# Edge copies of three batches on ScalarE, a new order of emission, and six fewer filler matmuls

## The chip, the core and the metric

The kernel runs on one core of a Trainium2 chip. The time is the device time of one launch in microseconds: the median of 3 runs. The engines of the core are TensorE (PE in the rows, with its weight loads as PEld), VectorE (DVE), ScalarE (ACT), GpSimd (POOL) and SyncE (SP), which issues most of the DMA transfers. Each engine works off its own list of instructions in order; between engines they wait for one another by semaphores.

## What is computed

Eight batches of eight heads, 512 tokens, 32 states and 64 columns to a head. Tokens attend to states and states to tokens; both results go through a feed-forward layer whose hidden values are gated by a convolution of width 3 along the tokens.

```python
scores = scale * np.matmul(x, state.transpose(0, 1, 3, 2))
a = softmax(scores)
xread = np.matmul(a, state)
scores2 = scale * np.matmul(state, x.transpose(0, 1, 3, 2))
a2 = softmax(scores2)
sread = np.matmul(a2, x)
x = np.concatenate([xread, sread], axis=2)      # 576 rows to a batch, 512 columns
...
h = np.maximum(x @ w_in, 0.0)                   # 576 x 1024
hp = h with one row of zeros on either side
for k in range(3):
    conv_out += conv_w[k][None, None, :] * hp[:, k:k + S, :]
gate = 1.0 / (1.0 + np.exp(-conv_out))
return h * gate @ w_out
```

## The kernel before

Hidden values are held with the 1024 columns on partitions, as eight blocks `f` of 128 for each batch `b`; a step `i` is one pair (`b`, `f`) of 512 tokens. For a step TensorE makes `ps_h` (`first_hidden` for batch 0, `hidden` for the others), `relu` copies it into the tile `h`, `middle` multiplies by the convolution's middle tap into `t`, two instructions of VectorE add the outer taps (`before`, `behind`), ScalarE takes tanh (`sigmoid`), VectorE gates (`gate`), `gate_high` and `gate_low` split the result into two parts for TensorE, and `project` adds them into `acc` with three matmuls to a 128-token chunk. `end` scales an `acc` into `o`, and `store` sends it off. All stores go on SP's queue but one, `LAST`, which goes on ScalarE's.

The 32 state rows of a batch stand behind its 512 tokens. They are computed for four batches at once: `state_tokens` fills `hs`, which holds them for each block with a column of space on either side. Two copies join the two parts: `join` copies the first state column behind the tokens of `h` (column 512), and `edge` copies the last token column in front of the states in `hs`. Both are 128x1 copies on GpSimd. Batch 0 comes before its states are there, so its very last token column is finished later: `edge` also keeps the last two columns of each block in `corner`, and `corner_taps`, `corner_sum` and what follows make the missing column, which is then in `last`. A buffer of `h` is free for a later step when `join`, `edge`, the taps and the gate of its step are through; there are five of them, and eight PSUM banks in all.

Batch 0 is also started in a shorter way: `first_scores` multiplies the states `st` (loaded by `state_load`, the first part on ScalarE's DMA queue) with the first half of the tokens `xt`, and then the second half; `keep_scores` keeps them, `first_flip` transposes them, `first_top` takes the maximum, and so on to `first_div`, before `first_hidden` can begin. Weights are rounded on ScalarE and VectorE as they come (`w_abs` to `w_sign`), the convolution's weights `conv_w` (the DMA of `w_load` on ScalarE's queue, then `raw` and `hc`) among the first.

`fill` is a matmul of zeros that nobody reads. What stands in which order is not computed in the kernel: every operation is added to a plan with what it reads and writes, and the table `ORDER` lists their numbers in the order in which they are emitted. A number -n stands for n calls of `fill`, and a number with a v for an operation that VectorE takes in place of ScalarE. Tile numbers in the lists below (`h_1098`) count the tiles as they are made.

Of the kernel before, what the change touches and what calls it, by code (L numbers as in the profile page):

```python
# [12 lines left out]
AF = mybir.ActivationFunctionType  # L13
# [3 lines left out]
B, H, S, NS, D = 8, 8, 512, 32, 64  # L17
# [28 lines left out]
LAST = (B - 1, 1, 1)  # L46
# [37 lines left out]
876 863 396 890 943v 864 738 891 973 877 1521 324 946 309 957 843 879 858 892 392 958 894 311 932 840 325 865 441 855  # L84
# [3 lines left out]
1044 1526 448 952 481 482 966 1527 479 475 1029v 937 480 477 1528 999 478 1030 941 940 923 1010 955 938 956 924 1529  # L88
# [6 lines left out]
1123 1138 1066 408 1094 1139v 1142 1140 1155 414 409 1067 1079 1168 1069 1068 1080 1537 1095 1082 1083 1158 1143 1107  # L95
1124 1539 1127v 1108 1144 1540 1169 1145 1146 1172 1159 1109 1170 1084 1097 1099 1098 1081 1110 1541 1251 374 1156 377
1173 1171 1141 1174 1125 1252 1126 1112 1114 1117v 378 375 1118 1147 1148 376 1542 1530 1128 1538 1266 1096 1113 1129
1160 1121 1130 1543 1161 1131 1175 1162 1111 1176 1183 1544 1132 1177 1267 1115v 1184 1198 1178 1187v 1199 1254 1202v
1201 1122 1203 1545 1133 1547 1213 1228 1546 1136 1200 1204 1255 1256 1548 1163 1205 1270 1137 1134 1149 1135 1253
1185 1188 1189 1206 1257 1549 1150 1152 1550 1258 1551 1190 1116 1119 1120 1191 1214v 1167 1192 1552 1182 1164 1151  # L100
1179 1166 1553 1181 1207 1217v 1216 1186 1193 1555 1215 1268 1229 1196 1165 1194 1296 415 1556 1259 1218 1232v 1271
1219 1208 1211 1272 1220 1297 1180 1209 1230 1233 1557 1558 1559 1560 1234 1554 1195 1221 416 418 1222 1273 1223 1561
1235 1281 1197 1210 1236 1300 1237 1282v 1231 1284 417 419 1274 1298 1238 1285 1212 1226 1224 1227 1225 1269 1240 1311
1241 1563 1275 449 1301 1302 1312 1299 1286 1283 1326 1242 1247 1287 1288 1248 1289 1356 1290 1303 1239 1315v 1276
1327v 1304 1260 1243 1341 1261 1342 1343 1357v 1313 1344 1314 1329 1358 1249v 1316 1244 456 1317 1564 1250 451 1359
1305 452 454 457 1565 1291 1263 1278 1264 1562 1279 1294 1566 455 1567 453 1568 1569 1330v 1345 1570 1346 450 459 1571
1572 1573 1360 1262 1318 1319 1277 1293 1292 1379 460 1361 1306 1574 1362 1575 1309 1265 1347 1280 1308 1576 1577 1380
1363 1381 458 1331 1364 1578 1584 1382 1328 1383 1320 1579 1332 1585 1384 1348 1333 1586 1321 1580 1582 1245v 1334
1587 1335 1588 1246 1581 1385 1424 1394 1295 1589 1386 1425 1336 1590 1387 1409 1349 1428 1307 1324 1429 1323 1310
1350 1410 1365 1351 1338 1325 1427 1411 1395v 1396 1340 1412 1397 1339 1366 1583 1322 1592 1593 1398 1413v 1399 1414  # L110
1594 1415 1416 1439 1595 1596 1597 1400 1426 1430 1598 1401 1440 1600 1441 1402 1601 1469 1337 1602 1603 1431 1388
1604 1591 1605 1432 1606 1389 1353 1454 1455 1484 1458v 1403 1417 1456 1485v 1459 1352 1354 1355 1393 1608 1609 1610
1404 1470v 1472 1599 1368 1370 1611 1607 1418 1392 1419 1460 1443 1612 1457 1444 1442 1613 1471 1473v 1373 1488 1369
# [46 lines left out]
def fused_kernel(ctx: ExitStack, tc: tile.TileContext, xT, xn, stT, w_in, conv_w, w_out, out):  # L160
# [478 lines left out]
    def relu(i, on=A):  # L639
        hd[i] = buf([P, S + 1], F32, "h", f"h_{i}")  # L640
        rectified(hd[i][:, :S], ps_h.pop(i), on)

    def join(i):
        b, f = at_step(i)
        m, j = PLACE[b]
        G.tensor_copy(hd[i][:, S:], hs[m, f][:, j, 1:2])  # L646
# [293 lines left out]
```

## Time and profile before

| | |
|---|---|
| median of 3 runs | 360.16 us (359.75 to 360.31) |
| the profiled execution | 359.77 us |
| its span in the trace | 358.0 us |
| outside the span | 1.77 us |
| instructions | 6754 |

The times compare whole launches; the rows of the profile stand within the span of the one profiled execution. The profile lists for each engine how long its instructions ran, in which stretch, and, in brackets, how long the engine had been idle before an instruction and which other instruction let it go on. Matmuls overlap with one another, so the time of a group of them is best read from its start to the start of the next group.

### The profile page before, as it was taken

To read this page: it belongs to the slowest core of one execution; us is meant where nothing else is said; L and a number is where in the kernel's file an instruction comes from. 1 tells how busy PE (TensorE), PEld (TensorE's weight loads), DVE (VectorE), ACT (ScalarE), POOL (GpSimd) and SP (SyncE) were. 2 spreads that over 40 slices of the span, in tenths; PEclk is the share of its full clock that TensorE was granted. 3 is DMA by queue.
4 is the path that set the end of the run, shared out by engine and by line. 5 is a ranking of instruction groups with operands and counts; after the bars stand their busy time and mean duration, and the time that the engine had idled before them with its cause. 6 is when DMAs were issued, how large, how long until landed. Compare 5 with 4: busy or idle time off the path is not lost.

```text
span 358.0 us, 6754 instructions
## 1 busy us (share of the span) xinstructions
PE 351.5 (98%) x2556; PEld 274.9 (77%) x2556; DVE 319.0 (89%) x566; ACT 251.0 (70%) x517; POOL 45.3 (13%) x144
## 2 busy tenths in 40 slices
PE   8999999999999999999999999999999999999995
PEld 6867667857778787878789886887887868888884
DVE  1999999989999999999999999998888699989850
ACT  3999999879768789668867469455746575755532
POOL 1012020152010102000101003030110210204000
PEclk9999999999999999999999999999999999999999
DMA  7999999500200014031600011001000020200114
GB/s 233 384 351 335 369 356 305 205 0 32 89 2 0 3 59 146 2 117 39 231 0 2 0 44 75 0 2 57 34 29 0 13 77 0 61 0 0 60 60 147
DMA packets 13584, 35.06 MB, mean 98 GB/s; under 512 B 1520, under 2 KB 4720, under 8 KB 12528
## 3 DMA queue, kind: packets, MB, share of 16 engines
q1 hardware_dynamic: 13120, 34.41, 26.9%
q8 instruction: 20, 0.33, 0.4%
q10 hardware_dynamic: 432, 0.22, 0.2%
q14 instruction: 12, 0.10, 0.1%
HBM read 25.71 MB, written 8.91 MB: 97 GB/s over the span
## 4 chain that ended last, share of the span: by engine, by line
PE 90%; ACT 5%; DMA 2%; POOL 1%; issue 0%; SPq 0%
PE acc L694 47%; PE ps_h L629 20%; PE ps_hs L614 4%; PE ps_u L547 4%; PE acc_t L694 3%; PE ps_r L367 2%; DMA xt<-xT 2%; PE ps_t L354 2%; PE acc_c L694 2%; PE acc L702 1%; POOL hs L651 1%; PE idle L214 1%; ACT h L199 1%; PE ps_s L309 1%; PE ps_h L636 1%; ACT t L193 1%
## 5 line engine op out<-in xcount | busy, mean ns | idle before, releaser
L694 PE MATMUL acc<-wo,g 128*128 128x512 f32 x726 | 178.1, 394 | 0.0
L694 PEld LDWEIGHTS acc<-wo,g 128*128 128x128 f32 x726 | 134.4, 188 | 33.4 <-issue 4.2
L629 PE MATMUL ps_h<-a,u 128*128 128x512 f32 x336 | 82.9, 391 | 0.0
L629 PEld LDWEIGHTS ps_h<-a,u 128*128 128x128 f32 x336 | 62.8, 188 | 13.9 <-ACT g L204 0.8
L651 POOL COPY hs<-h 128x1 f32<-128x1 f32 x64 | 26.2, 423 | 224.4 <-ACT h L199 183.4
L671 ACT ACTIVATE t<-t 128x512 f32<-128x512 f32 x64 | 39.5, 633 | 20.9 <-DVE t L667 20.7
L667 DVE SCALAR_TENSOR_TENSOR t<-h,cw,t 128x512 f32<-128x512 f32 (+1 forms) x64 | 47.3, 745 | 1.3
L662 DVE SCALAR_TENSOR_TENSOR t<-h,cw,t 128x511 f32<-128x511 f32 x64 | 47.0, 743 | 0.5 <-ACT t L193 0.5
L676 DVE SCALAR_TENSOR_TENSOR t<-t,h 128x512 f32<-128x512 f32 (+1 forms) x64 | 41.9, 668 | 5.4 <-ACT t L671 5.3
L199 ACT ACTIVATE h<-ps_h 128x512 f32<-128x512 f32 x55 | 32.4, 594 | 18.7 <-PE ps_h L629 16.5
L204 ACT ACTIVATE g<-t 128x512 fp32r<-128x512 f32 (+1 forms) x62 | 38.0, 618 | 10.1 <-DVE t L676 8.5
L207 DVE TENSOR_TENSOR g<-t,g 128x512 fp32r<-128x512 f32 (+1 forms) x62 | 41.4, 672 | 2.3 <-ACT g L204 2.1
L193 ACT ACTIVATE t<-h,cw 128x512 f32<-128x512 f32 x53 | 37.8, 723 | 2.4 <-DVE g L207 1.3
L646 POOL COPY h<-hs 128x1 f32<-128x1 f32 x56 | 17.3, 330 | 61.4 <-DVE t L676 31.2
L204 ACT ACTIVATE u<-ps_u 128x512 fp32r<-128x512 f32 x28 | 16.4, 602 | 4.9 <-PE ps_u L547 4.9
L708 ACT ACTIVATE o<-acc 128x512 f32<-128x512 f32 (+1 forms) x27 | 14.6, 548 | 7.3 <-PE acc L694 5.9
L207 DVE TENSOR_TENSOR u<-ps_u,u 128x512 fp32r<-128x512 f32 x28 | 19.0, 683 | 0.5 <-ACT u L204 0.5
L547 PE MATMUL ps_u<-wi,st 64*32 64x512 f32 x224 | 16.0, 598 | 0.3 <-ACT h L199 0.3
L614 PEld LDWEIGHTS ps_hs<-sr,wi 128*128 128x128 f32 x128 | 14.8, 192 | 1.1 <-ACT o L708 0.8
L636 PE MATMUL ps_h<-p,u 128*128 128x256 f32 x64 | 15.4, 386 | 0.0
L614 PE MATMUL ps_hs<-sr,wi 128*128 128x128 f32 x128 | 15.0, 276 | 0.0
L636 PEld LDWEIGHTS ps_h<-p,u 128*128 128x128 f32 x64 | 11.7, 190 | 3.7 <-issue 1.3
(96 smaller groups left out, 401.0 us busy)
## 6 DMA issues: line engine op xcount, KB each, us to landing
xt<-xT SPq DMA_DIRECT2D x16, 512.0 KB, 7.6
xx<-xn SPq DMA_DIRECT2D x8, 1024.0 KB, 6.5
out<-o SPq DMA_DIRECT2D x27, 256.0 KB, 2.0
raw<-w_in SPq DMA_DIRECT2D x8, 512.0 KB, 7.7
raw<-w_out SPq DMA_DIRECT2D x8, 512.0 KB, 7.4
out<-o SPq DMA_DIRECT2D x7, 128.0 KB, 1.8
out<-o_t SPq DMA_DIRECT2D x8, 64.0 KB, 1.7
st<-stT SPq DMA_DIRECT2D x1, 448.0 KB, 10.7
```

What stands on the lines that cost most here:

```text
L193: A.activation(dst, src, AF.Copy, scale=scale)
L199: A.activation(dst, src, AF.Relu, scale=0.5)
L204: A.activation(hi, src, AF.Copy)
L207: engine.tensor_tensor(lo, src, hi.bitcast(F32), op=ALU.subtract)
L614: PE.matmul(ps_hs[m, f][:, :NT], wi[:, k, f * P:(f + 1) * P], sr[m][:, k, :], start=(k == 0), stop=(k == NK - 1))
L629: PE.matmul(ps_h[i], u[j][:, g, fs], a[k][:, g, :], start=(n == 0), stop=(n == 3 * NG - 1))
L636: PE.matmul(ps_h[f][:, q * HS:(q + 1) * HS], us[0, f // 4][0][:, g, f % 4 * P:(f % 4 + 1) * P], half_of(pa[0], q)[:, g, :], start=(g == 0) ...
L662: V.scalar_tensor_tensor(t[:, 1:], h[:, :S - 1], cw[:, f, 0:1], t[:, 1:], op0=ALU.mult, op1=ALU.add)
L667: V.scalar_tensor_tensor(t[:, :n], h[:, 1:n + 1], cw[:, f, 2:3], t[:, :n], op0=ALU.mult, op1=ALU.add)
L671: A.activation(tt[i], tt[i], AF.Tanh, scale=0.25)
L676: V.scalar_tensor_tensor(tt[i][:, :n], tt[i][:, :n], 1.0, hd[i][:, :n], op0=ALU.add, op1=ALU.mult)
L694: PE.matmul(acc, g[j][:, cs], wo[:, k, f, :], start=(f == 0 and n == 0), stop=(f == NF - 1 and n == 2))
```

## The change

`join` and `edge` of the batches 0 to 2 (`EARLY`) run on ScalarE as activations with the function Copy. For batch 0 `edge` keeps only the two `corner` columns; the copies into `hs` that it made before are made for all eight blocks at once by `first_edges` on GpSimd, as one 128x8 copy, and `corner_taps` is one such copy too. `LAST` names another store. The table `ORDER` is replaced throughout; its numbers behind step 7 are larger by one, for the new operation. The sum of its negative numbers goes from 25 to 19. Counted over the whole program, some work changes engine between ScalarE and VectorE by the table's v and by the order: VectorE has 2 in place of 0 of the four first `keep_scores` (128x256), 12 in place of 9 `relu`, 15 in place of 11 `middle`, and 4 in place of 6 whole evacuations `o`; ScalarE has the complement of each.

```diff
-LAST = (B - 1, 1, 1)
+LAST = (B - 1, 0, 0)
+
+EARLY = 3
...
 ORDER = """
-0 98 99 101 100 102 120 -9 123 121 -3 124 125 103 142 2 143 126 -2 150 127 4 3 151 5 132 20 21 23 144 152 8 22 6 24
...
+98 100 99 101 0 102 120 -9 123 121 103 -3 124 125v 126 -1 142 143 127 2 -1 150 3 151 5 132 4 144 6 152 20 128 130 21
...
+    def moved(dst, src, b):
+        if b < EARLY:
+            A.activation(dst, src, AF.Copy)
+        else:
+            G.tensor_copy(dst, src)
+
     def join(i):
         b, f = at_step(i)
         m, j = PLACE[b]
-        G.tensor_copy(hd[i][:, S:], hs[m, f][:, j, 1:2])
+        moved(hd[i][:, S:], hs[m, f][:, j, 1:2], b)
 
     def edge(i):
         b, f = at_step(i)
         m, j = PLACE[b]
-        G.tensor_copy(hs[m, f][:, j, :1], hd[i][:, S - 1:S])
         if b == 0:
-            G.tensor_copy(corner[:, f, :2], hd[i][:, S - 2:S])
+            moved(corner[:, f, :2], hd[i][:, S - 2:S], b)
+        else:
+            moved(hs[m, f][:, j, :1], hd[i][:, S - 1:S], b)
+
+    def first_edges():
+        G.tensor_copy(every[:, :NF, 0, 0], corner[:, :, 1])
...
     def corner_taps():
-        for f in range(NF):
-            G.tensor_copy(corner[:, f, 2:], hs[0, f][:, 0, 1:2])
+        G.tensor_copy(corner[:, :, 2], every[:, :NF, 0, 1])
...
+        copies = ("ACT", "small") if b < EARLY else ("POOL", "pool")
         if b:
-            add("POOL", "pool", partial(join, i), r=[("hs", m, f), h], w=[("h2", i)])
-        add("POOL", "pool", partial(edge, i), r=[h], w=[("edge", i)] + ([("corner", f)] if b == 0 else []))
+            add(*copies, partial(join, i), r=[("hs", m, f), h], w=[("h2", i)])
+        add(*copies, partial(edge, i), r=[h], w=[("edge", i)] if b else [("corner", f)])
+        if i == NF - 1:
+            add("POOL", "pool", first_edges, r=[("corner", f) for f in range(NF)] + [("hs", 0, f) for f in range(NF)],
+                w=[("edge", f) for f in range(NF)])
```

ScalarE's list at its start, before (`st` are the states, `raw` and `hc` the convolution's weights, `at` the first scores):

```order
L880 DMA st<-stT 128x128
L238 DMA raw_92<-conv_w 128x48
L242 ACT_TABLE_LOAD
L242 ACTIVATE hc_94<-raw_92 128x24
L245 ACTIVATE raw_92<-raw_92 128x24
L193 ACTIVATE at_111<-ps_s_0_0_112 128x256
L193 ACTIVATE at_111<-ps_s_0_1_113 128x256
L193 ACTIVATE at_111<-ps_s_1_0_127 128x256
```

and the same list in the changed kernel:

```order
L240 DMA raw_91<-conv_w 128x48
L247 ACT_TABLE_LOAD
L247 ACTIVATE raw_91<-raw_91 128x24
L244 ACTIVATE hc_94<-raw_91 128x24
L895 DMA st<-stT 128x128
L195 ACTIVATE at_111<-ps_s_1_0_128 128x256
L195 ACTIVATE at_111<-ps_s_1_1_129 128x256
```

The load of `st` has moved from the first place behind the two activations that read `conv_w`, and the first two copies of scores have left for VectorE.

GpSimd's list where the copies of batch 0 end and those of batch 1 begin, before (`h_1067` is the first step of batch 1 in this list, `h_696`, `h_698` and `h_667` are of batch 0):

```order
L651 COPY hs<-h_698 128x1
L653 COPY corner<-h_698 128x2
L651 COPY hs<-h_1067 128x1
L651 COPY hs<-h_696 128x1
L653 COPY corner<-h_696 128x2
L769 COPY corner<-hs 128x1 x8
L651 COPY hs<-h_667 128x1
L653 COPY corner<-h_667 128x2
```

and GpSimd's list of the changed kernel from the last instruction of its start on:

```order
L182 TENSOR_SCALAR eight<-ident 128x128
L665 COPY hs<-corner 128x8
L780 COPY corner<-hs 128x8
L649 COPY hs<-h_1876 128x1
L649 COPY h_1876<-hs 128x1
```

Before the first copies of batch 3 (`h_1876`) GpSimd has only the two 128x8 copies left.

ScalarE's list at the same place, before (each `h` takes its buffer from an earlier step):

```order
L204 ACTIVATE g_5_1080<-t_960 128x384
L199 ACTIVATE h_1086<-ps_h_1073 128x512
L204 ACTIVATE wo<-whole_1054 128x512
L199 ACTIVATE h_1098<-ps_h_1088 128x512
L671 ACTIVATE t_1012<-t_1012 128x512
L204 ACTIVATE wo<-whole_648 128x512
```

and in the changed kernel, at the last of the eight copies of batch 0:

```order
L201 ACTIVATE h_1073<-ps_h_1018 128x512
L620 ACTIVATE hs<-ps_hs_6_966 128x4x32
L647 ACTIVATE corner<-h_663 128x2
L244 ACTIVATE hc_1108<-raw_1096 128x512
L206 ACTIVATE wo<-whole_714 128x512
L206 ACTIVATE wo<-whole_1069 128x512
```

The copy of the edge now stands in ScalarE's own list, where before the next `relu` of that list stood behind a copy on GpSimd.

## Rows read from the trace of the kernel before

**Rows 1.** The page's first part: busy time, share of the span and instructions of each engine.

```profile
PE 351.5 (98%) x2556; PEld 274.9 (77%) x2556; DVE 319.0 (89%) x566; ACT 251.0 (70%) x517; POOL 45.3 (13%) x144
```

**Rows 2.** Busy time by stretch: the stretch and its length, then for each engine its busy us and instructions, the granted TensorE clock, the share of the DMA engines' time and GB/s.

```profile
20.60:70.00 49.40, 48.81 (x567) 36.23 (x560) 47.05 (x94) 47.27 (x107) 5.75 (x12) 1.00 0.92 331
70.00:78.00 8.00, 7.71 (x54) 4.30 (x53) 6.65 (x14) 5.86 (x12) 6.12 (x14) 1.00 0.00 0
78.00:130.00 52.00, 52.00 (x337) 39.68 (x336) 51.53 (x83) 42.42 (x82) 4.79 (x22) 1.00 0.07 27
130.00:340.00 210.00, 210.00 (x1248) 167.92 (x1247) 195.39 (x335) 136.20 (x275) 27.30 (x88) 1.00 0.12 43
```

**Rows 3.** The timeline from 70 to 78 us: start, us, engine, line, operation, tiles, shape, count, and in brackets the idle time before it and what ended that.

```profile
70.49 4.70 POOL L651 COPY hs<-h 128x1 f32<-128x1 f32 x2 [19.01 <-ACT h L199]
...
74.46 0.68 DVE L207 TENSOR_TENSOR wo<-whole,wo 128x512 fp32r<-128x512 f32 x1
...
74.68 1.02 PE L547 MATMUL ps_u<-wi,st 64*32 64x512 f32 x2
...
75.12 0.19 POOL L653 COPY corner<-h 128x2 f32<-128x2 f32 x1
...
75.34 0.60 ACT L199 ACTIVATE h<-ps_h 128x512 f32<-128x512 f32 x1 [1.80 <-POOL corner L653]
...
75.99 1.09 PE L547 MATMUL ps_u<-wi,st 64*32 64x512 f32 x14 [0.29 <-ACT h L199]
...
76.49 0.56 DVE L676 SCALAR_TENSOR_TENSOR t<-t,h 128x384 f32<-128x384 f32 x1 [1.35 <-ACT t L671]
...
77.01 1.20 PE L694 MATMUL acc<-wo,g 128*128 128x512 f32 x4
```

**Rows 4.** The timeline from 121 to 123 us, TensorE: the same 16 state products later, and the group behind them.

```profile
121.11 1.09 PE L547 MATMUL ps_u<-wi,st 64*32 64x512 f32 x16
...
122.13 1.20 PE L629 MATMUL ps_h<-a,u 128*128 128x512 f32 x4
```

**Rows 5.** Statistics of GpSimd's copies over the run: shortest, median and longest in ns, first and last start. The second row is that of the eight copies of `corner_taps`.

```profile
L651 POOL COPY hs<-h x64: 178/185/4002, 23.6 to 329.5; 128x1 f32<-128x1 f32 x64
...
L769 POOL COPY corner<-hs x8: 177/178/178, 75.2 to 76.1; 128x1 f32<-128x1 f32 x8
```

**Rows 6.** The timeline of the first 9 us.

```profile
0.72 0.38 ACTq L880 DMA_DIRECT2D st<-stT  x1
...
1.03 4.21 PE L214 MATMUL idle<-zeros 128*128 128x128 f32 x18 [1.03 <-DVE zeros L176]
1.14 0.45 ACTq L238 DMA_DIRECT2D raw<-conv_w  x1
...
4.90 0.22 ACT L242 ACTIVATE hc<-raw 128x24 f32<-128x24 f32 x1 [2.00 <-DMA raw<-conv_w]
5.03 0.21 ACT L245 ACTIVATE raw<-raw 128x24 uint32<-128x24 uint32 x1
...
5.41 0.67 PE L319 MATMUL ps_s<-xt,st 64*32 64x256 f32 x16 [0.16 <-DMA xt<-xT]
...
6.00 0.94 PE L214 MATMUL idle<-zeros 128*128 128x128 f32 x6
...
7.35 0.67 PE L319 MATMUL ps_s<-xt,st 64*32 64x256 f32 x16 [0.41 <-DMA xt<-xT]
...
8.64 0.69 DVE L491 TENSOR_REDUCE m<-ps_x 128x16 f32<-128x512 f32 x1 [2.58 <-PE ps_x L487]
```

**Rows 7.** DMA issues on ScalarE's queue: count, KB each, us from issue to landing.

```profile
st<-stT ACTq DMA_DIRECT2D x1, 64.0 KB, 3.0
raw<-conv_w ACTq DMA_DIRECT2D x1, 24.0 KB, 3.7
```

**Rows 8.** The timeline from 11.5 to 21 us: VectorE's wait behind the sums of the first exponentials, and TensorE's first hidden product.

```profile
14.92 0.17 DVE L515 TENSOR_SCALAR s<-ps_x 128x16 f32<-128x16 f32 x1 [0.35 <-PE ps_x L511]
...
20.59 0.70 PE L636 MATMUL ps_h<-p,u 128*128 128x256 f32 x2
```

**Rows 9.** The timeline from 36 to 41 us.

```profile
37.76 0.73 PEld L636 LDWEIGHTS ps_h<-p,u 128*128 128x128 f32 x4 [0.84 <-ACT raw L245]
...
39.47 1.10 PE L367 MATMUL ps_r<-xx,e2t 128*32 128x64 f32 x64 [0.59 <-ACT at L193]
```

**Rows 10.** Groups of instructions by line and shape: busy us, mean ns of one, and the idle time before them with what ended it.

```profile
L193 ACT ACTIVATE t<-h,cw 128x512 f32<-128x512 f32 x53 | 37.8, 723 | 2.4 <-DVE g L207 1.3 <-DVE h L201 0.9
L199 ACT ACTIVATE h<-ps_h 128x512 f32<-128x512 f32 x55 | 32.4, 594 | 18.7 <-PE ps_h L629 16.5 <-POOL corner L653 1.8 <-PE ps_h L636 0.4
...
L201 DVE TENSOR_SCALAR h<-ps_h 128x512 f32<-128x512 f32 x9 | 6.2, 686 | 0.9 <-PE ps_h L629 0.9
...
L195 DVE TENSOR_SCALAR t<-h,cw 128x512 f32<-128x512 f32 x11 | 5.3, 483 | 0.6 <-ACT h L199 0.6
...
L193 ACT ACTIVATE at<-ps_s 128x256 f32<-128x256 f32 x4 | 1.3, 380 | 2.2 <-PE ps_s L319 2.2
...
L710 DVE TENSOR_SCALAR o<-acc 128x256 f32<-128x256 f32 x2 | 0.8, 420 | 4.7 <-PE acc L694 4.7
```

**Rows 11.** The timeline of the last 4 us, ScalarE's evacuations and its store.

```profile
354.08 0.66 ACT L708 ACTIVATE o<-acc 128x256 f32<-128x256 f32 x2 [1.20 <-PE acc L694]
...
354.77 0.36 ACTq L729 DMA_DIRECT2D out<-o  x1
```

More of the change, by code (lines that the diff above doesn't have):

```diff
@@ L56 @@
 ORDER = """
[27 rows of a table removed]
-876 863 396 890 943v 864 738 891 973 877 1521 324 946 309 957 843 879 858 892 392 958 894 311 932 840 325 865 441 855
[3 rows of a table removed]
-1044 1526 448 952 481 482 966 1527 479 475 1029v 937 480 477 1528 999 478 1030 941 940 923 1010 955 938 956 924 1529
[6 rows of a table removed]
-1123 1138 1066 408 1094 1139v 1142 1140 1155 414 409 1067 1079 1168 1069 1068 1080 1537 1095 1082 1083 1158 1143 1107
-1124 1539 1127v 1108 1144 1540 1169 1145 1146 1172 1159 1109 1170 1084 1097 1099 1098 1081 1110 1541 1251 374 1156 377
-1173 1171 1141 1174 1125 1252 1126 1112 1114 1117v 378 375 1118 1147 1148 376 1542 1530 1128 1538 1266 1096 1113 1129
@@ L98 @@
[L98 to L112, printed above, removed]
@@ L113 @@
-1404 1470v 1472 1599 1368 1370 1611 1607 1418 1392 1419 1460 1443 1612 1457 1444 1442 1613 1471 1473v 1373 1488 1369
-1408 1391 1487 1486 1445 1446 1407 1489 1614 1461 1624 1423 1390 1405 1422 1420 1367 1447 1490 1625 1615 1626 1627
-1628 1629 1433 1630 1462 1616 1617 1434 1438 1618 1406 1619 1377v 1620 1621 1491 1378 1374 1474 1475 1622 1435 1421
-1437 1448 1463 1623 1449 1464 1450 1631 1492 1632 1476 1477 1633 1478 1634 1375 1635 1436 1636 1465 1453 1468 1637
-1452 1638 1376 1639 1467 1493 1640 1641 1494 1479 1642 1371v 1643 1644 1483 1645 1372 1646 1498 1511 1482 1647 1497
@@ L118 @@
-1451 1480 1509 1648 1512 1510 1650 1651 1649 1495 1499v 1513 1507v 1501 1514 1508 1502 1652 1500 1466 1481 1496 1503
-1504 1505 1506
+98 100 99 101 0 102 120 -9 123 121 103 -3 124 125v 126 -1 142 143 127 2 -1 150 3 151 5 132 4 144 6 152 20 128 130 21
[3 rows of a table added]
+137 536 537 504 158 138 159 470 161 494 472 207 519v 471 538 162 520 213 208 590 545 62 63 163 212 495 521 546 575 591
[22 rows of a table added]
+931 860 921 395 959 960 310 392 903 933 891 922 892 881 311 900 880 306 944 312 930 904 962v 973 934 861 863 326 441
[9 rows of a table added]
+1051 1105v 1055 1124 1052 1091 1077 414 1063 1540 1541 1064 1092 1542 1125 1078 1065 1139 1140 1066 1079 1142 1141
@@ new lines @@
+1093 1039 1154 1054 1106 1080 1081 412 1094 1107 1095 1155 1053 1070 1169 1068 1170v 1158v 1096 1157 1126 1127 1108
+1128v 1543 408 1171 1104 374 1129 1069 1083 1067 1173 1159 1156 375 377 1174 378 1175 1109 1130 1110 1131 1098 1084
+1544 1111 1082 409 1132 376 1545 1546 1097 1085 1099 1100 1143 1114 1144 1115 1112 1145 1116v 991 1117 1146 1548 1549
+1184 1550 1133 1176 1551 1552 1160 1185 1134 1229 1161 1199 1214 1122 449 1200v 1177 1203v 1147 1113 1148 1123 1215
+1553 1162 1216 1149 1118v 1554 1163 1252 1188 1230v 1164 1556 1178 1187 1202 1179 1297 1136 1135 415 1151 1172 1201
@@ new lines @@
+1186 1298v 1218v 1219 1220 1204 1150 1165 418 1547 1557 1189 1555 1558 416 1221 1120 1121 1190 1233v 1119 1217 1191
+1559 1137 1152 1167 1166 417 1222 1253v 1205 419 1256 1299 1254 1560 1234 1561 1206 1231 1267 1138 1153 1192 1257 1562
+1207 1235 1168 1181 1182 1183 1268 1193 1180 1258 1236 1282 1194 1283 1270 1232 1312 1208 1271v 1237 1209 1300 1286v
+1313v 1314 1238 1255 1285 1284 1223 1239 1224 1272 1269 1197 1273 1287 1288 1274 1564 1275 1198 1565 1566 1196 1327
+1213 1195 1567 1259 1289 1210 1212 1225 1276 1240 1316 1317 1228 1243 1342 1211 1568 1260 1226 1227 1357 1563 1261
@@ new lines @@
+1244 450 1343v 1262 1290 1328 1331 1277 1245 1263 1250 1569 1358 1251 1361v 1362 1291 1570 1301 1302 1303 1292 451
+1329 1330 1344 1572 1315 1345 1359 456 1242 454 452 455 1248 1573 453 1574 1332 1363 1241 457 459 1571 1575 1265 1278
+1304 1346v 1576 1246 1305 1306 1577 1280 1264 1293 1395 1347 1307 1295 1380 1578 460 1318 1381v 1585 1319 1320 1382
+1383 1586 1384 1385 1425 1266 1310 1247 1587 1348 1333 1386 1281 458 1364 1321 1334 1335 1349 1588 1589 1322 1350
+1426v 1279 1351 1294 1296 1579 1308 1410 1311 1309 1326 1411v 1590 1396v 1427 1429 1365 1591 1336 1580 1366 1583 1412
@@ new lines @@
+1398 1323 1592 1593 1387 1352 1430 1337 1428 1399v 1388 1594 1431 1414 1415 1595 1596 1581 1325 1324 1340 1339 1455
+1397 1360 1354 1355 1597 1338 1367 1598 1416 1389 1353 1249 1413 1599 1440 1601 1417 1390 1602 1368 1370 1400 1603
+1604 1441 1442 1401 1418 1605 1369 1606 1456 1459 1432 1444v 1607 1376v 1377 1582 1445 1458 1609 1402 1470 1471 1610
+1472 1473 1443 1611 1392 1433 1341 1600 1608 1393 1612 1446 1356 1447 1374 1613 1460 1614 1448 1485 1457 1419 1371
+1403 1615 1616 1391 1625 1461 1626 1404 1627 1394 1628 1629 1462 1405 1630 1407 1408 1406 1631 1617 1420 1618 1619
@@ new lines @@
+1375 1486v 1488 1422 1409 1424 1620 1434 1463 1435 1474v 1378 1621 1439 1423 1437 1464 1449 1622 1465 1623 1624 1633
+1438 1450 1452 1634 1635 1475 1421 1632 1436 1379 1487 1636 1637 1638 1639 1489 1451 1640 1453 1490 1641 1454 1584
+1491 1469 1642 1476 1492 1643 1493 1477 1644 1478 1645 1646 1647 1479 1494 1648 1372v 1649 1652 1650 1467 1468 1495
+1480 1373 1653 1466 1483 1482 1497 1651 1504 1498 1484 1506 1510v 1505 1511 1499 1508 1514v 1512 1507 1515 1513 1481
+1496 1509 1502 1500 1503 1501
```

69 rows, old and new, of the table ORDER are left out of this document.

## The prediction

> **What bounds the kernel now.** The engine totals come first [rows 1]: TensorE is busy in 98% of the span and VectorE in 89%, so a change of this kind can win only where TensorE stands, or where a run of its matmuls takes longer than its size asks for. The table by stage [rows 2] shows how little visible standing there is: after the first hidden product, which starts at 20.59 us [rows 8], TensorE is busy 48.81 of 49.40 us, then 7.71 of 8.00, then without a gap to 340. VectorE is just as full up to 130 us (51.53 of 52.00) and has 210.00 - 195.39 = 14.6 us free between 130 and 340. So TensorE sets the end, and VectorE, which prepares its operands, sets how early TensorE can go on in the first third. GpSimd, ScalarE after 70 us and the DMA queues after 70 us have room.
>
> A "busy" TensorE can hide a wait, so the next view is the timeline of the one stage where TensorE, VectorE and ScalarE all have gaps, 70 to 78 us [rows 3]. Two one-element-wide copies on GpSimd start at 70.49 and last until 75.19. The columns of such a copy are tiny, and the statistics of that line say what is normal: 185 ns in the median, 4002 ns at the longest [rows 5]. The next GpSimd copy, at 75.12, is what ScalarE's `relu` at 75.34 waited for (1.80 us idle). That `relu` gives a PSUM bank back: TensorE's group of 16 state products begins at 74.68 with 2 matmuls and goes on with the other 14 only at 75.99; the next group starts at 77.01, 2.33 us after the first matmul. The same group elsewhere needs 122.13 - 121.11 = 1.02 us [rows 4]. So TensorE lost 2.33 - 1.02 = 1.31 us there, though the waits show only 0.29. VectorE idles at the same place: its last instruction ended at 74.46 + 0.68 = 75.14 and the next, at 76.49, waited 1.35 us for ScalarE's tanh, which stands behind that `relu`. TensorE, VectorE and ScalarE all lose some 1.3 us to one late GpSimd copy.
>
> **What the rows say about the slow copy, and a rule.** It ran while VectorE worked without a gap, and it ended when VectorE stopped at 75.14 [rows 3]; the eight copies right after it, with VectorE idle, took 178 ns each [rows 5]. I take it that VectorE's back-to-back work holds GpSimd off. The Trainium skill, GPSIMD Engine Reference, section 1 (Specifications), says that GpSimd shares its SBUF interfaces with VectorE, and that an instruction of VectorE with two SBUF inputs or in a two-port mode contends with it. By that rule, the trace agrees (4002 against 185 ns), and the two copies left on GpSimd early in the new kernel could be held in the same way; what that would cost is the third rival below.
>
> **The change part by part, against the profiled execution of 359.77 us** (span 358.0; the median of the runs is 0.39 above it, at 360.16).
>
> *The copies.* Forty small copies, those of batches 0 to 2, go from GpSimd to ScalarE, and the eight `corner` copies and eight `hs` copies of batch 0 on GpSimd become two copies of 128x8. The `relu` at 75.34 then waits for no GpSimd copy: of the stall, TensorE gets 1.31 us back and VectorE 1.35. I take **-1.4 us** with bounds -1.8 (the 1.80 that ScalarE waited) and -1.3. On ScalarE a small copy costs between 0.13 us (the start of the 128x24 instruction at 4.90 to the next at 5.03) and its full 0.22 us [rows 6]: 40 copies make 5.2 to 8.8 us. Against that, ScalarE hands work of 2 x 0.38 + 4 x 0.723 + 1 x 0.594 = 4.25 us to VectorE (two halves of the first scores, four middle taps, and three `relu` less two evacuations of the same size) [rows 10], so it carries about 1 to 4.6 us more over the whole run. In the stages after 78 us ScalarE has 10 us free in 52 and 74 us in 210 [rows 2]; that cover hides the copies there, and only 8 of the 40 belong to the stage before. I cost them at **0**, with +0.5 as the upper bound, where `relu`s stand a few copies later.
>
> *VectorE's extra work.* The same moves give VectorE 2 x 0.42 + 4 x 0.483 + 1 x 0.686 = 3.46 us more [rows 10]. After 130 us its 14.6 us of free time cover that. Ahead of the first gated chunks of batch 2 the order lists hold only one extra tap (0.48) and the two score copies (0.84). The score copies run in the 2.58 us for which VectorE waits for the first flip [rows 6]; without that cover they would cost their 0.84 in full. The tap is on the path, since VectorE is full there. I take **+0.5**, bounds +0.3 and +1.0; the second is what the queue ahead of the chunks of batch 1 grows by if the order around it also packs worse.
>
> *Fewer multiplications for nobody.* The fills fall from 25 to 19; the first twelve stay, and the thirteen behind the second scores become seven, in places where TensorE waits anyway. Three of them, of two matmuls each, take 0.94 us at 6.00 [rows 6], 0.31 each. Six less would be 1.9, but most fill a wait that stays. VectorE waited for TensorE behind such fills at 14.92, for 0.35 us [rows 8]. I take **-0.3**, bounds 0 and -0.9 (the 0.35 and two fills, where TensorE could have gone on).
>
> *The short waits near 38 us.* ScalarE is late there twice: TensorE's loads wait 0.84 us at 37.76 and its matmuls stand 0.59 us at 39.47 [rows 9]. In the new order ScalarE has less work queued ahead of those two places, but VectorE and the loads are full there as well (DMA share 0.92 in that stage, [rows 2]). **-0.3**, bounds 0 and -1.0.
>
> *The tail.* The last matmuls end at 354.08; two evacuations of 0.66 us together and ScalarE's own store at 354.77 follow [rows 11]. The changed kernel ends with the same pair on ScalarE and one store on its queue, for another chunk. **0**, give or take 0.3: seven of the eight last stores still share SP's queue.
>
> The sum is -1.4 + 0.5 - 0.3 - 0.3 = -1.5 us, of which I keep -1.4 for the copies' cost on ScalarE: 359.77 - 1.4 = 358.4 profiled, **358.8 us** on the scale of the median.
>
> **The rivals.** *First: VectorE catches the gain.* Once the stall is gone, TensorE asks 1.3 us earlier for operands of an engine that has only 0.47 us free in the 52 us behind it [rows 2]. VectorE gains its 1.35 us too, which speaks against this; for it speaks that it also gets new work in front of the chunks. If its extra work costs 1.0 and the start and the waits near 38 us give nothing, -1.4 + 1.0 = -0.4, and with ScalarE's +0.5 it is +0.1: 359.8 to 360.3, and 359.5 to 360.5 with the tail's 0.3: the same.
>
> *Second, on the slower side: the load of the first states is held.* In the kernel before, ScalarE's queue issues the `st` load first, at 0.72, and `conv_w` at 1.14; they land after 3.0 and 3.7 us [rows 6, 7]. In the new order `conv_w` comes first and the `st` load stands behind the two activations that wait for it. If that wait holds the queue, `conv_w` lands at 0.72 + 3.7 = 4.4, the load issues at 4.7 and lands at 7.7 to 8.4, and the first scores, now at 5.41, start there. Both scores, the flips and fills behind them then end 2 to 2.6 us later: what now is VectorE's first wait, at 8.64, ends near 10.8. VectorE is full from there, so nearly all of it stays. After a stand TensorE also starts slowly: the first 18 matmuls of fills took 4.21 us, 0.23 each, where six at 6.00 took 0.94, 0.16 each [rows 6]; on the 32 score matmuls, the flips and the fills that is up to 1.1 us more. 358.8 + 2.1 to 358.8 + 3.7 is 360.9 to 362.5. It decides from the point where `st` lands later than the second `xt`, at 7.35 [rows 6]; a load issued by 2.5 costs nothing. No row of the trace shows a DMA of ScalarE's queue behind a waiting activation. The Trainium skill, Perfetto Trace Analysis, section "DVE / Act Engine Instruction", has the sequencer push an instruction into a wait queue, where the semaphore is waited for, and go on with the next: by that the load would issue at about 2 us. No run here shows it, so both stay open.
>
> *Third: the remaining GpSimd copies are starved.* Two 128x8 copies must come ahead of VectorE's sum of the corner; at 4.0 us [rows 5] each, VectorE could wait. But VectorE's standing is what frees GpSimd, so this costs some 0.5 to 1 us: 359.3 to 359.8. What lets GpSimd go on is read off the rows above; the page named there only gives it a reason.
>
> **How the numbers follow.** Measurements of this kernel can tell 0.2%, 0.72 us, from no change. The forecast (358.2 to 359.4) gets 0.52, a better case (under 358.2, when the start gives its 0.9 and the waits near 38 us go) 0.08. The gain caught gets 0.18 and the starved copies 0.04, mostly within 0.2%. The held load gets 0.15, and 0.03 stays for the slow start of TensorE, as in the second rival but through fewer fills, also slower (near 361). That is faster 0.60, same 0.22, slower 0.18. The range of 8 in 10 leaves out half of the better case and most of the held load: **357.7 to 361.0**; the likeliest case alone spans 358.2 to 359.4.
>
> **What would show it.** Right: no GpSimd instruction over 1 us before 100 us; the `relu` groups wait for TensorE and not for GpSimd; every group of 16 state products takes some 1.0 us; first hidden product near 20.3; last matmul near 352.7. The first rival shows as VectorE without a gap over 0.5 us from 40 to 130 us and TensorE's loads waiting for `g`. The second shows at once: `st` on ScalarE's queue after 4 us, first scores after 7 us. Wrong would be a last matmul at 354 or later with the stall gone: then the stall was paid for by what VectorE had to do anyway.

## The result: 0.85% slower, and the profile after

| | before | changed |
|---|---|---|
| median of 8 runs | 359.90 us | 362.94 us (361.88 to 364.35) |
| ratio to before | | 1.0085 (95%: 1.0060 to 1.0111) |
| span of the profiled execution | 358.0 us | 360.4 us |

The forecast was 358.8 us with a range up to 361.0. The loss lies in the first 14 us. The timeline of the changed kernel's start (columns as in rows 6) answers to [rows 6] and [rows 8]:

```profile
0.72 0.38 ACTq L240 DMA_DIRECT2D raw<-conv_w  x1
...
1.13 1.28 ACT L247 ACT_TABLE_LOAD   x1 [1.13 <-PEq L947]
...
2.43 0.23 ACT L247 ACTIVATE raw<-raw 128x24 uint32<-128x24 uint32 x1
2.44 0.33 ACTq L895 DMA_DIRECT2D st<-stT  x1
...
9.23 1.11 PE L321 MATMUL ps_s<-xt,st 64*32 64x256 f32 x16 [3.99 <-DMA st<-stT]
...
10.27 1.65 PE L216 MATMUL idle<-zeros 128*128 128x128 f32 x6
...
13.76 0.69 DVE L493 TENSOR_REDUCE m<-ps_x 128x16 f32<-128x512 f32 x1 [2.39 <-PE ps_x L489]
...
24.91 1.35 PE L638 MATMUL ps_h<-p,u 128*128 128x256 f32 x5
```

The states `st` are issued at 2.44 in place of 0.72. TensorE stands 3.99 us for them, and the first scores start at 9.23 in place of 5.41. VectorE's first maximum comes at 13.76 in place of 8.64, the first hidden product at 24.91 in place of 20.59: 4.3 us late. The DMA view of the changed kernel (columns as in rows 7) shows that the later issue explains only 1.72 us of it:

```profile
st<-stT ACTq DMA_DIRECT2D x1, 64.0 KB, 6.7
raw<-conv_w ACTq DMA_DIRECT2D x1, 24.0 KB, 1.7
```

In [rows 7] the states took 3.0 us and `conv_w` 3.7. The load that is issued first, at 0.72 us, is the quicker one in both kernels. The other one meets SP's loads, which begin at 0.72 too, and in the changed kernel it comes 1.3 us later than `conv_w` did before (2.44 against 1.14).

The stages of the changed kernel (columns as in rows 2) show the second part of the loss:

```profile
8.00:14.00 6.00, 4.77 (x49) 3.05 (x50) 1.19 (x4) 1.02 (x3) 0.00 (x0) 0.72 1.06 390
...
70.00:78.00 8.00, 8.00 (x55) 5.78 (x61) 8.00 (x17) 8.00 (x21) 1.32 (x2) 1.00 0.55 199
```

After its stand of 4 us TensorE's granted clock is 0.72 in the mean from 8 to 14 us, that is, part of that time at the lower of its two levels: the 16 score matmuls took 1.11 us there (0.67 before) and six fills 1.65 (0.94 before). In the stage of the old stall, 70 to 78 us, TensorE is now busy 8.00 of 8.00, against 7.71 in [rows 2]. The group of state products that had taken 2.33 us there takes 77.67 - 76.78 = 0.89 us again; the timeline of the changed kernel, TensorE and GpSimd, answers to [rows 3]:

```profile
76.68 0.88 POOL L665 COPY hs<-corner 128x8 f32<-128x8 f32 x1 [74.73 <-ACT corner L647]
77.50 1.06 POOL L780 COPY corner<-hs 128x8 f32<-128x8 f32 x1
...
76.78 1.09 PE L549 MATMUL ps_u<-wi,st 64*32 64x512 f32 x16
77.67 1.06 PE L311 MATMUL ps_s<-xt,st 64*32 64x512 f32 x16
```

At the end the two kernels do the same thing: the pair on ScalarE starts at 356.82, and 360.4 - 356.82 = 3.6 us remain, against 358.0 - 354.08 = 3.9 before [rows 11].

### The profile page after: what moved, and what is told of

It is laid out like the page before. It is cut to its first block, busy times and chain, and to the rows that moved or that the text cites. A ratio compares the mean times of both kernels' runs of the same rounds, so it can differ in the third digit from the quotient of the medians.

```text
span 360.4 us, 6703 instructions
## 1 busy us (share of the span) xinstructions
PE 351.0 (97%) x2544; PEld 274.0 (76%) x2544; DVE 320.4 (89%) x573; ACT 251.3 (70%) x550; POOL 32.5 (9%) x90
## 4 chain that ended last, share of the span: by engine, by line
PE 89%; DMA 4%; DVE 4%; ACT 2%; issue 1%; ACTq 0%
PE acc L706 44%; PE ps_h L631 20%; PE ps_hs L616 4%; PE ps_u L549 4%; PE ps_h L638 3%; PE acc_t L706 3%; DMA xx<-xn 2%; PE ps_r L369 2%; DMA st<-stT 2%; PE ps_t L356 2%; PE ps_s L311 2%; PE acc_c L706 2%; PE idle L216 1%; PE acc L714 1%; PE ps_u L568 1%
## 5 line engine op out<-in xcount | busy, mean ns | idle before, releaser
L683 ACT ACTIVATE t<-t 128x512 f32<-128x512 f32 x64 | 40.4, 640 | 20.5 <-DVE t L679 20.5
L201 ACT ACTIVATE h<-ps_h 128x512 f32<-128x512 f32 x52 | 31.6, 610 | 17.9 <-PE ps_h L631 16.4
L195 ACT ACTIVATE t<-h,cw 128x512 f32<-128x512 f32 x49 | 35.6, 728 | 3.0 <-DVE h L203 2.4
L649 POOL COPY hs<-h 128x1 f32<-128x1 f32 x40 | 17.5, 458 | 164.0 <-ACT h L201 151.3
L720 ACT ACTIVATE o<-acc 128x512 f32<-128x512 f32 (+1 forms) x29 | 15.5, 549 | 7.3 <-PE acc L706 5.8
L649 POOL COPY h<-hs 128x1 f32<-128x1 f32 x40 | 13.5, 350 | 64.9 <-DVE t L688 59.8
L195 ACT ACTIVATE at<-ps_s 128x512 f32<-128x512 f32 (+1 forms) x16 | 9.7, 624 | 10.2 <-PE ps_s L321 10.2
L549 PE MATMUL ps_u<-wi,st 64*32 64x512 f32 x224 | 14.8, 598 | 0.0
```

What stands on the lines that cost most here:

```text
L195: A.activation(dst, src, AF.Copy, scale=scale)
L201: A.activation(dst, src, AF.Relu, scale=0.5)
L649: G.tensor_copy(dst, src)
L683: A.activation(tt[i], tt[i], AF.Tanh, scale=0.25)
```

## The experiments

Each run is told by its ratio to the kernel before that ran on the same chip, with the 95% interval, and its median.

### The place of the st load

`st_first`: the load of the states first again, all else as changed.

```diff
-98 100 99 101 0 102 120 -9 123
+0 98 100 99 101 102 120 -9 123
```

> The changed kernel with one move undone: the load of the first states st is again the first instruction of ScalarE's queue, ahead of conv_w. Theory A (the changed kernel is slow because st, issued 1.72 us later and behind 1 MB of xt, lands 6.1 us later; the rest of the change is a gain): first scores back near 5.4 us, clock 1.0 throughout the start, 358.5 to 359.2 us, 0.995 to 0.998 of before. Theory B (the start is late, but the rest of the change gains nothing, since VectorE has no room for it): first scores near 5.4 as well, but 359.7 to 360.5 us, 1.000 of before.

Measured: 357.87 us, 0.9951 (0.9925 to 0.9976). Its DMA view and its timeline:

```profile
st<-stT ACTq DMA_DIRECT2D x1, 64.0 KB, 2.0
...
5.17 1.11 PE L321 MATMUL ps_s<-xt,st 64*32 64x256 f32 x16
...
6.21 1.20 PE L216 MATMUL idle<-zeros 128*128 128x128 f32 x6
...
8.89 0.69 DVE L493 TENSOR_REDUCE m<-ps_x 128x16 f32<-128x512 f32 x1 [1.57 <-PE ps_x L489]
...
20.04 2.21 PE L638 MATMUL ps_h<-p,u 128*128 128x256 f32 x9
```

One number moved in the table gives back 362.94 - 357.87 = 5.1 us. The rest of the change is a gain of 2.0 us (359.91 of the kernel before on the same chip to 357.87; by the interval 0.9 to 2.7 us), so theory B falls. The median is below the 358.5 to 359.2 us that theory A named.

`st_second`: directly behind `conv_w`, ahead of the table load.

```diff
-98 100 99 101 0 102 120 -9 123
+98 0 100 99 101 102 120 -9 123
```

> The changed kernel with the st load directly behind the conv_w load on ScalarE's queue, ahead of the table load and the two activations. It issues near 1.15 us. Theory A1 (what matters is how much of xt is ahead of it in the transfers): it lands near 4.5 to 5 us, as conv_w did before in that place (issued 1.14, 3.7 to landing), and the scores start at 5.4 to 5.6: within 0.3 us of st_first. Theory A2 (any load behind xt takes some 6.7 us): it lands near 7.8, the scores start at 7.9, 361 to 362 us.

Measured: 357.78 us, 0.9950 (0.9933 to 0.9967), with this landing:

```profile
st<-stT ACTq DMA_DIRECT2D x1, 64.0 KB, 3.9
```

Issued at 1.14, it lands at 5.0, in time for the scores at 5.36. Theory A2, that any load behind `xt` is as late as in the changed kernel, falls. Between an issue at 1.14 and one at 2.44 lie 1.3 us, and 4.1 us of landing time.

`before_st_late`: that move alone, in the kernel before.

```diff
-0 98 99 101 100 102 120 -9 123
+98 99 101 100 0 102 120 -9 123
```

> The kernel before with that one move alone: on ScalarE's queue conv_w, the table load and the two activations come ahead of the st load; all else as before. Theory A: st lands near 9 us, first scores near 9.2, TensorE at half clock for some 3 us, and 3.8 to 4.6 us more than before: 1.010 to 1.013. Theory B says the same of the start, but would let some of it be caught up later: under 1.008.

Measured: 364.60 us, 1.0137 (1.0117 to 1.0156): 4.7 us, a little over the range named. Its DMA view, its timeline and its stage from 8 to 14 us:

```profile
st<-stT ACTq DMA_DIRECT2D x1, 64.0 KB, 5.8
raw<-conv_w ACTq DMA_DIRECT2D x1, 24.0 KB, 1.8
...
0.72 0.39 ACTq L238 DMA_DIRECT2D raw<-conv_w  x1
1.14 1.28 ACT L242 ACT_TABLE_LOAD   x1 [1.14 <-PEq L932]
2.54 0.22 ACT L242 ACTIVATE hc<-raw 128x24 f32<-128x24 f32 x1
2.54 0.33 ACTq L880 DMA_DIRECT2D st<-stT  x1
...
8.44 1.11 PE L319 MATMUL ps_s<-xt,st 64*32 64x256 f32 x16 [3.20 <-DMA st<-stT]
9.48 1.65 PE L214 MATMUL idle<-zeros 128*128 128x128 f32 x6
...
8.00:14.00 6.00, 5.56 (x49) 3.75 (x50) 0.75 (x2) 2.40 (x7) 0.00 (x0) 1.00 1.05 377
```

The states land at 2.54 + 5.8 = 8.3, earlier than the 9 us expected.

`loads_behind_st`: every load from ScalarE's queue, so that only `conv_w` is ahead of the states and nothing of SP's beside them.

```diff
-            nc.sync.dma_start(xts[i], xT[b, :, :, g * HS:(g + 1) * HS])
+            nc.scalar.dma_start(xts[i], xT[b, :, :, g * HS:(g + 1) * HS])
...
-        (nc.scalar if j == W_CONV else nc.sync).dma_start(raws[j], pieces[j][0].bitcast(U32).rearrange("p k (n t) -> p k n t", t=2))
+        nc.scalar.dma_start(raws[j], pieces[j][0].bitcast(U32).rearrange("p k (n t) -> p k n t", t=2))
...
-        (nc.sync if i else nc.scalar).dma_start(st[:, parts[i], :], stT[:, parts[i], :])
+        nc.scalar.dma_start(st[:, parts[i], :], stT[:, parts[i], :])
```

(`xx` and the later `xt` likewise.)

> The changed kernel with every load issued from ScalarE's queue, so that st, issued near 2.44 us as in the changed kernel, has only conv_w ahead of it and no transfer of SP's beside it; slow as a whole, since ScalarE then issues all loads in its order. Theory A1 (xt in front of and beside st makes it land late): st lands 2 to 3 us after its issue, as when it was issued first. Theory A2 (a load behind another one on ScalarE's queue, or behind the table load, lands late by itself): 5.8 to 6.7 us as in the changed kernel.

Measured: 434.3 us in a single run, as a whole of no use; its DMA view:

```profile
st<-stT ACTq DMA_DIRECT2D x1, 64.0 KB, 1.9
```

The issue was at 2.57, behind the table load as in the changed kernel. Without SP's transfers the same load lands in 1.9 us in place of 6.7. So the late landing is SP's loads, ahead of it and beside it. How the states stood in line shows in the DMA view of the changed kernel, from 2.5 to 5.7 us and then from 5.7 to 8.8 us (queue; packets, MB, share of the 16 engines' time; q1 is SP's queue, q10 ScalarE's):

```profile
q1 hardware_dynamic: 885, 0.88, 85.9%
...
q1 hardware_dynamic: 706, 0.82, 83.4%
q10 hardware_dynamic: 144, 0.07, 8.4%
```

After the issue at 2.44 no packet of ScalarE's queue runs until 5.7 us, while SP's queue moves 0.88 MB; then the states' packets run for some 3 us beside SP's.

### The clock

`fills_to_cover`: the states as late as in the changed kernel, but 18 more fills in front of the first scores.

```diff
-98 100 99 101 0 102 120 -9 123
+98 100 99 101 0 102 120 -27 123
```

> The changed kernel with 27 in place of 9 fills ahead of the first scores, so that TensorE has work until st lands; the states are as late as in the changed kernel. If the half clock from 8.5 to 11.9 us costs on the path: clock 1.0 over the start, first flip's maximum on VectorE 1.1 to 1.7 us earlier than 13.76, and 361.2 to 361.9 us against 362.9. If only the late landing counts: within 0.4 us of the changed kernel.

Measured: 360.55 us, 1.0028 (1.0010 to 1.0047), 2.4 us under the changed kernel. Its timeline and its stage from 8 to 14 us:

```profile
1.03 7.85 PE L216 MATMUL idle<-zeros 128*128 128x128 f32 x54 [1.03 <-DVE zeros L178]
...
8.82 0.66 PE L321 MATMUL ps_s<-xt,st 64*32 64x256 f32 x16
...
11.83 0.69 DVE L493 TENSOR_REDUCE m<-ps_x 128x16 f32<-128x512 f32 x1 [1.50 <-PE ps_x L489]
...
8.00:14.00 6.00, 5.77 (x98) 4.23 (x101) 2.92 (x7) 2.61 (x7) 0.00 (x0) 1.00 1.01 368
```

The scores start only 0.4 us earlier than in the changed kernel, the first maximum 1.9, a little more than expected, and the time is below the range named. The granted clock stays at 1.00. From the first scores to the first maximum it is 11.83 - 8.82 = 3.0 us, against 13.76 - 9.23 = 4.5 in the changed kernel: 1.5 us of the gain are the quicker matmuls, and 0.4 the earlier landing. But `st_first`, which has no stand, also begins slowly (1.11 us for the scores, 1.20 for the fills) and takes 8.89 - 5.17 = 3.7 us. So the 2.4 us are what the extra fills give, and not what the stand costs: of the 4.9 us between the first maxima of the changed kernel and of `st_first`, 9.23 - 5.17 = 4.1 are the late scores and 0.8 the slower matmuls behind the stand.

The row of the granted clock does not tell the pace by itself. In `before_st_late` it stands at 1.00 from 8 to 14 us, and the scores and fills are as slow as in the changed kernel (1.11 and 1.65 us). Nor does it fall only after a stand. In the profiled execution of `st_second`, TensorE is busy from 14 to 20.6 us without a gap at a mean of 0.74, and 64 matmuls take 3.33 us; the last line is the same group in `st_first`:

```profile
14.00:20.60 6.60, 6.60 (x124) 5.19 (x124) 6.26 (x17) 4.96 (x12) 0.00 (x0) 0.74 1.02 396
...
15.23 3.33 PE L499 MATMUL ps_x<-ident,s 128*32 128x128 f32 x64
...
15.68 1.95 PE L499 MATMUL ps_x<-ident,s 128*32 128x128 f32 x64
```

What set off that fall the runs don't show.

### The copies

`before_copies`: the copies of batches 0 to 2 on ScalarE, in the old order.

```diff
+    def moved(dst, src, b):
+        if b < 3:
+            A.activation(dst, src, AF.Copy)
+        else:
+            G.tensor_copy(dst, src)
...
-        G.tensor_copy(hd[i][:, S:], hs[m, f][:, j, 1:2])
+        moved(hd[i][:, S:], hs[m, f][:, j, 1:2], b)
...
-        G.tensor_copy(hs[m, f][:, j, :1], hd[i][:, S - 1:S])
+        moved(hs[m, f][:, j, :1], hd[i][:, S - 1:S], b)
...
-            G.tensor_copy(corner[:, f, :2], hd[i][:, S - 2:S])
+            moved(corner[:, f, :2], hd[i][:, S - 2:S], b)
```

> The kernel before, in its own order, with the copies of batches 0 to 2 on ScalarE (all 48, those into hs of batch 0 one by one); nothing else changed. If the one held GpSimd copy at 70.49 us is what TensorE loses there, the group of 16 state products at 74.7 takes 1.0 us and the time falls by 1.3 to 2.0 us: 0.9945 to 0.9965. If ScalarE, full from 20 to 70 us, pays for 16 copies there at 0.13 us each, up to 2.1 us of that is lost again: 0.997 to 1.001. If VectorE has no room for the gain: 0.999 to 1.001 with the stall gone.

Measured: 360.26 us, 1.0016 (0.9996 to 1.0035): no gain. The stall of TensorE is gone from its timeline, and yet a GpSimd copy is held longer than ever, one of `corner_taps`, for which no `relu` waits. Its timeline, first TensorE, then VectorE, and the statistics of that line of GpSimd (shortest, median, longest in ns):

```profile
20.27 1.99 PE L636 MATMUL ps_h<-p,u 128*128 128x256 f32 x8
...
48.18 1.29 PE L367 MATMUL ps_r<-xx,e2t 128*32 128x64 f32 x64 [0.55 <-DMA xx<-xn]
...
56.56 1.10 PE L367 MATMUL ps_r<-xx,e2t 128*32 128x64 f32 x64 [0.22 <-DMA xx<-xn]
...
76.12 1.06 PE L547 MATMUL ps_u<-wi,st 64*32 64x512 f32 x16
77.12 1.20 PE L700 MATMUL acc<-wo,g 128*128 128x512 f32 x4
...
79.42 0.69 DVE L207 TENSOR_TENSOR wo<-whole,wo 128x512 fp32r<-128x512 f32 x1
80.89 0.18 DVE L778 TENSOR_TENSOR corner<-corner,cw 128x24 f32<-128x24 f32 x1 [0.78 <-POOL corner L775]
...
L775 POOL COPY corner<-hs x8: 178/178/7552, 72.4 to 80.7; 128x1 f32<-128x1 f32 x8
```

The copy of 7.55 us, the second of the eight, began at 72.6, while VectorE worked without a gap. VectorE's last instruction before its wait ends at 79.42 + 0.69 = 80.11; then the copy is through, and the six behind it take some 178 ns each. This is the mechanism of the prediction's third rival, with its price, 0.78 us, on VectorE. The group of 16 again takes 77.12 - 76.12 = 1.0 us. But it starts 76.12 - 74.68 = 1.4 us later than in the kernel before [rows 3], although the first hidden product came 0.3 us earlier (20.27 against 20.59, [rows 8]): what the stall gave back had been lost on the way. Two waits for loads of `xx`, of 0.55 and 0.22 us, are part of it. The rest falls where ScalarE is full [rows 2] and has the added copies, as the second expectation has it, but no single wait shows it.

`st_first_pool`: `st_first` with the moved copies back on GpSimd; `st_second_pool` is the same on `st_second`.

```diff
-EARLY = 3
+EARLY = 0
```

> st_first (the new order, st loaded first) with all of the moved copies back on GpSimd. If GpSimd is held off by VectorE's work whatever the order, one of its copies takes over 1 us between 25 and 90 us, a relu waits for it and the time is 0.7 to 2 us above st_first's 357.9. If the stall of the kernel before was a coincidence of its order, GpSimd is no worse here: within 0.4 us of st_first.

> st_second (st directly behind conv_w) with the moved copies back on GpSimd. A second look at what the copies cost in the new order: if the 0.7 us by which st_first_pool was under st_first is the copies on ScalarE, 0.4 to 1.0 us under st_second's 357.8; if it is spread between runs, within 0.3 us of it.

Measured: 357.18 us, 0.9924 (0.9902 to 0.9947), and 357.01 us, 0.9931 (0.9909 to 0.9954). Both are 0.7 to 0.8 us under their fellows with the copies on ScalarE. The intervals of each pair overlap, so the size is uncertain; that the move brings nothing in this order is plain. The statistics of GpSimd's copies in `st_first_pool`, and a line of its timeline:

```profile
L649 POOL COPY h<-hs x56: 177/184/1387, 72.2 to 330.7; 128x1 f32<-128x1 f32 x56
L649 POOL COPY hs<-h x56: 177/184/1820, 73.2 to 330.2; 128x1 f32<-128x1 f32 x56
...
L649 POOL COPY corner<-h x8: 179/412/715, 22.9 to 53.5; 128x2 f32<-128x2 f32 x8
...
78.54 1.84 POOL L649 COPY hs<-h 128x1 f32<-128x1 f32 x2 [5.11 <-ACT h L201]
```

The eight copies of batch 0 take at most 0.715 us. GpSimd is still held at times (the two copies at 78.54 take 1.84 us), but no `relu` waits for it: the stall belonged to the old order, which asked for a copy just where VectorE had no gap and a `relu` stood behind it. The 0.7 us need not be the copies: most of what separates the profiled executions of `st_first` and `st_first_pool` (spans of 356.0 and 355.1 us) is a wait of 0.72 us for a load at 55 us (shown in the next section), which `st_first_pool` does not have.

### Fills, VectorE's share, the tail

`st_first_fills`: the six fills put back, at six of the seven single ones; the first line of the table as an example.

```diff
-0 98 100 99 101 102 120 -9 123 121 103 -3 124 125v 126 -1 142 143 127 2 -1 150 3 151 5 132 4 144 6 152 20 128 130 21
+0 98 100 99 101 102 120 -9 123 121 103 -3 124 125v 126 -2 142 143 127 2 -2 150 3 151 5 132 4 144 6 152 20 128 130 21
...
```

> st_first with the six fills that the change left out put back, one more at six of the seven places behind the second scores. If a fill there is on the path: 0.3 to 1.0 us above st_first's 357.9, the first hidden product later by that than 20.04. If they stand in waits of TensorE: within 0.3 us.

Measured: 358.44 us, 0.9952 (0.9932 to 0.9972). The median is 0.6 us above `st_first`, the ratio the same: not told apart. The first hidden product starts at 20.80, 0.8 us later than in `st_first`; but in the profiled execution of `st_first` that lead was lost at 55 us to a load. The first line is of `st_first_fills`, the second of `st_first`:

```profile
20.80 3.72 PE L638 MATMUL ps_h<-p,u 128*128 128x256 f32 x16
...
54.92 1.10 PE L369 MATMUL ps_r<-xx,e2t 128*32 128x64 f32 x64 [0.72 <-DMA xx<-xn]
```

`st_first_no_v`: what the table gives to VectorE goes back to ScalarE, the first scores apart: every v but that of 125 is struck out; the first line with one as an example.

```diff
-137 536 537 504 158 138 159 470 161 494 472 207 519v 471 538 162 520 213 208 590 545 62 63 163 212 495 521 546 575 591
+137 536 537 504 158 138 159 470 161 494 472 207 519 471 538 162 520 213 208 590 545 62 63 163 212 495 521 546 575 591
...
```

> st_first with every operation that the table gives to VectorE in ScalarE's place taken back to ScalarE (33 of 34; the first scores stay): relu, middle taps and evacuations, some 18 us less on VectorE and 20 us more on ScalarE. If the work that the change adds to VectorE costs the 0.5 us of the sum, or lets part of the gain be caught between 75 and 290 us: 0.3 to 1.0 us under st_first's 357.9. If that work stands in VectorE's free time: within 0.4 us, or slower, where a relu on ScalarE then comes late.

Measured: 360.19 us, 1.0012 (0.9996 to 1.0027), 2.3 us slower than `st_first`. In the view of waits from 225 to 300 us (engine and line, the line waited for, us in total, times, longest), of this kernel and then of `st_first`, VectorE now waits for ScalarE's middle taps:

```profile
DVE t L674 <- ACT t L195: 8.2, 6, 2.8
```

```profile
DVE t L674 <- ACT t L195: 2.6, 1, 2.6
```

`st_first_last`: the old choice of the store on ScalarE's queue.

```diff
-LAST = (B - 1, 0, 0)
+LAST = (B - 1, 1, 1)
```

> st_first with the store on ScalarE's queue that the kernel before had (second half of chunk 1, no longer the last to be evacuated), so that the last store of all stands on SP's queue behind six others. If the tail is set by the last store's issue and landing: 0.3 to 1.5 us above st_first's 357.9, as SP issues one store in some 0.5 us. If the pair on ScalarE sets it anyway: within 0.3 us.

Measured: 358.64 us, 0.9983 (0.9962 to 1.0004), 0.8 us over `st_first` by the medians and 0.3% by the ratios, with intervals that overlap. From the last pair on ScalarE to the end of the span it is 3.65 us, and 3.62 in `st_first`: the profiled executions don't show the loss. The mean granted clock is 0.995 or less in 8 of these 12 runs, against 3 of 12 of `st_first`, so the loss may be the clock; the tail stays open within some 0.8 us.

## Why the prediction was wrong, point by point

- **The step that failed is the bound of the second rival: "a load issued by 2.5 costs nothing".** On this bound the sum had no term for the start of the states' load. The rival added the 3.0 to 3.7 us of the loads issued at 0.72 and 1.14 to any issue time. The load was issued at 2.44 and took 6.7 us, since SP's loads were under way; alone behind `conv_w` it took 1.9. [Rows 7] had the sign of it: `conv_w`, less than half as large as the states and issued 0.42 us later, took 0.7 us longer. I read these two landings as fixed durations of two loads, when they were places in a queue of transfers.
- **The rival had the right load and the wrong durations.** It let the wait for `conv_w` hold the queue until 4.7, with the 3.7 us that `conv_w` took in second place. In first place it took 1.7 and landed at 2.4, just as the table load of 1.28 us ahead of the activations ended (1.13 + 1.28), and the states were issued 0.01 us behind the first activation. There the two causes can't be told apart. In `before_st_late` they can, by a little: the table load ends at 1.14 + 1.28 = 2.42, `conv_w` lands at 0.72 + 1.8 = 2.5, and the activation and the issue both come at 2.54. So the wait did hold the issue, for some 0.1 us. By the rule of the Trainium skill (Perfetto Trace Analysis, "DVE / Act Engine Instruction"), that the sequencer goes on past a waiting instruction, the issue need not have waited for it. The Trainium skill, DMA: Bandwidth & Descriptors, section "Queues, rings and completion order", says that each DMA engine takes turns between the queues at packet granularity; by that 64 KB would not have to wait for whole loads of another queue. The trace agrees from 5.7 us on, where the two queues run side by side, and not before, where 0.88 MB of SP's went first. Why, the runs don't show.
- **The slow matmuls after the stand were sized about right.** I allowed up to 1.1 us for them. From the first scores to the first maximum it is 4.5 us in the changed kernel, 3.7 in `st_first` and 8.64 - 5.41 = 3.2 before [rows 6], so they cost 0.8 to 1.3 us. What the rival had too small is the landing, at 9.1 in place of 7.7 to 8.4.
- **The term for the copies, -1.4 us, was right for the stall, and the change of engine was not needed for it.** With the copies back on GpSimd the new order has no such stall and is no slower (0.9924 and 0.9931); in the old order the move alone takes the stall away and gives nothing (1.0016). The cost of the copies on ScalarE, taken at 0 with a bound of +0.5, may be 0.2 to 0.3% in the new order (some 0.7 us). That is not told apart from the spread.
- **VectorE's extra work, +0.5 us, is not sized.** Taking all such work off VectorE cost 2.3 us: it took lateness off ScalarE. But that experiment strikes out 33 marks v, where the change only raised them from 28 to 34, so it shows neither the size nor the sign of the term.
- **The rest of the change** is worth 2.0 us by the medians, where the forecast had -1.4. Between the profiled executions of the kernel before and of `st_first`, whose spans differ by 2.0 us, the first hidden product comes 0.55 us earlier (20.04 against 20.59), the wait of 0.59 us near 38 us [rows 9] and the 1.31 us of the stall are gone, and the wait of 0.72 us at 55 us is new: -1.7 us. By these rows the terms for the fills and for the waits near 38 us (-0.3 each) were too small and a late load was not foreseen, so that the sum came near in part by luck. The new choice of the last store may hold up to 0.8 us of it. The first rival, VectorE catching the gain, falls with `st_first`.

The account of the changed kernel is: +5.1 us for the late states, of which some 0.8 are slower matmuls after the stand, and -2.0 us for everything else. Both are measured against `st_first`, so that their sum, 3.1 us, meets the 3.0 us measured by construction and is no test of the account. The lowest median was that of `st_second_pool`, at 357.01 us: the new order, the states loaded in good time, the copies on GpSimd; it is not told apart from `st_first_pool` (357.18).

## What to carry to other kernels

A landing time read from a trace belongs to a place in the order of all transfers: before a load is moved back, look at which transfers of other queues start in between, and take the landing of the load that stood in that place. When a whole table of order is replaced, read its first ten rows on every engine first; a load that everything waits for weighs more there than a stall of 1.3 us in the middle. A stall that one slow copy causes can be a coincidence of the order, so test the move alone before crediting it. And when fills cover a stand, compare with a run that has no stand: they can give more than the stand had cost.

## What was not expected of the hardware

A copy of 128x1 on GpSimd took 7.55 us while VectorE worked without a gap, and ended when VectorE stood still; its median is 178 ns. A 64 KB load took 1.9 to 3.0 us with no large load ahead of it, 3.9 us when issued 0.42 us after SP's first load, and 5.8 to 6.7 us when issued 1.7 to 1.8 us after it. The matmuls behind a stand of TensorE of 4 us cost 0.8 us more than those of `st_first`; in one run they were that slow with a granted clock of 1.00 in the row.
